# The diagonal of a linear-attention score block as eight products of its own, with a re-ordered start, hand-over and end

## The chip, the cores and the metric

The kernel runs on one core of one Trainium2 chip. The metric is the device time of one execution in microseconds (us), of the core; lower is better. PE is TensorE (PEld its weight loads), DVE VectorE, ACT ScalarE, POOL GpSimd, SP SyncE, which issues nearly all DMAs here.

## The reference

Two stages. The first is a recurrent attention with decay, over 4 batches, 8 heads, 768 steps and head width 48:

```
for t in range(S):
    cur = einsum('bhd,bhe->bhde', u * k[t], v[t])
    y[t] = einsum('bhd,bhde->bhe', r[t], state + cur)
    state = w * state + einsum('bhd,bhe->bhde', k[t], v[t])
```

The second is a mixture of eight experts on the 3072 x 384 result x. A token takes part where `x @ w_skip > 0`; its expert e is the largest of `x @ w_gate`, its weight g the softmax value there:

```
out = x;   out[tokens of e] += g * (relu(x @ w1[e]) @ w2[e])      # w1: 384 x 1024, w2: 1024 x 384
```

## The kernel before

**Attention.** The 768 steps are cut into 12 chunks of 64; two batches go together, so there are 24 steps `n` (two passes of 12), each with 8 heads as four pairs (`hp`) of two halves (`a`) of the 128 partitions, and two batches (`q`). Step `n` needs `dm[n]` (r and k, 512 KB) and `vz[n]` (v), both loaded on SP. DVE multiplies r by decay powers (`prep_r`, L412, writes `rd`), POOL multiplies k by the inverse powers (`prep_k`, L430, writes `kd`). The scores inside a chunk are `kd` against `rd`: below the diagonal with decay, on the diagonal with `u` in place of the decay. For the diagonal, `rd` holds a second copy of r that is multiplied by `uw` (u times w): two head pairs of it by DVE (L420), two by ACT (`bonus`, L406). `scores` (L442) makes 16 products of 64 x 64 weights and 128 moving columns: 64 for the copy below the diagonal, 64 for the diagonal's. Of the latter only the diagonal entries are used. Two predicated copies put both into `am`: L463 (`below`), L464 (`eye`).

A pass of the main loop (L890 on), for index `n`, writes in this order, which is the order on each engine: loads of `dm[n+5]`, `v[n+4]` and a piece of expert weights; `scores(n+1)`; the two masks; `across(n+1)` (L528, state against `rd`); a split of a weight piece (L115 on ACT, then L116 on POOL); `bonus(n+2)`; `turn_k(n+2)` (L455, transposes of `kd`); `turn_x(n)` (L571); `prep_k(n+3)`; a step or more of the routing (small DVE work); `prep_r(n+3)`; `state(n+1)` (L475); `within(n+1)` (L504, `am` against v); `evac(n+1)`, whose output goes back to DRAM on SP. Ahead of the loop the same is written out for steps 0 to 2, with `grow` (L325) making the powers for three more chunk positions, one of them on POOL.

**Routing and experts.** The router (`route`) sorts tokens into two lists of ids for each expert, 128 and 104 long (CAP = 232), in four groups of steps; the last group (`last`) can be done only after the last chunk. `gather(q)` (L124, indirect DMA on POOL) fetches a list's rows, `scatter(q)` (L174) writes them back. Weights are split into two parts, `hi` (ACT, L115) and `lo` (DVE or POOL, L116), and each product is made three times. Expert 0's two lists are run by `single`, a generator with 12 parts, so that they can be mixed into other work: `first` (list 0) is begun while the routing ends, `second` (list E) follows once gathered. The string `PLAN` gives the order: `a` a part of `first`, `B` a part of `second`, `x` the transposes of one list of expert 1, `s` a split, `u` a piece of expert 1, `g` a gather. `mix` (L171) adds an expert's result to its rows. Experts 1 to 7 are then run whole by `expert`.

**End.** Two flags are read on every engine (L1086, L1087) and two branches stand one behind the other (L1088, L1090) over code that is run only for unusual inputs.

Of the kernel before, what the change touches and what calls it, by code (L numbers as in the profile page):

```python
# [61 lines left out]
def tile_wkv_moe(  # L62
# [110 lines left out]
    def scatter(q):  # L173
        ins = nc.gpsimd.indirect_dma_start(  # L174
            out=out,
            out_offset=bass.IndirectOffsetOnAxis(ap=sid[:, q : q + 1], axis=0),
            in_=xs.pop(q),
            in_offset=None,
            bounds_check=N - 1,
            oob_is_err=False,  # L180
        )
# [64 lines left out]
    with ExitStack() as actx:  # L246
# [7 lines left out]
        def warm(k):  # L254
            for _ in range(k):
                nc.tensor.matmul(ps_t, ones[:, :P], ones, start=True, stop=True)
# [146 lines left out]
        def bonus(n, first=0):
            for hp in range(first, NHP):
                rd = rds[n][:, hp]
                nc.scalar.mul(rd[:, :, 1], rd[:, :, 0], uw[:, hp : hp + 1])  # L406

        def prep_r(n, parts=(0, 1)):
# [1 line left out]
            if 0 in parts:  # L410
                rds[n] = wk.tile([DR, NHP, 2, 2, C], F32, tag="rd", name=f"rd{n}", bufs=4)
                nc.vector.tensor_tensor(  # L412
                    rds[n][:, :, :, 0],
                    d[:, 0],
                    w_d[:, n % NSUB, 0][:, :, None].to_broadcast([DR, NHP, 2, C]),
                    ALU.mult,
                )
            if 1 in parts:
                rd = rds[n]
                nc.vector.tensor_tensor(  # L420
                    rd[:, :BH, :, 1],
                    rd[:, :BH, :, 0],
                    uw[:, :BH, None, None].to_broadcast([DR, BH, 2, C]),
                    ALU.mult,
                )
# [11 lines left out]
        def scores(n):  # L437
            kd, rd = kds.pop(n), rds[n]
            for hp in range(NHP):
                for a, q in FOUR:  # L440
# [1 line left out]
                    nc.tensor.matmul(  # L442
                        ps_p[q * C : (q + 1) * C, a, 2 * hp * C : 2 * (hp + 1) * C],
                        kd[h, hp, q, :],
                        rd[h, hp, q].rearrange("p s c -> p (s c)"),
# [13 lines left out]

        def mask_scores(n):  # L460
            p = ps_p.rearrange("p a (h s c) -> p (a h) s c", s=2, c=C)
            shape = lambda t: t.rearrange("p a (h c) -> p (a h) c", c=C)
            nc.vector.copy_predicated(shape(am[n % 2]), below, p[:, :, 0])  # L463
            nc.vector.copy_predicated(shape(am[n % 2]), eye, p[:, :, 1])  # L464
# [853 lines left out]
```

## Time and profile before

| | us |
|---|---|
| three runs | 267.34, 269.15, 269.96; median 269.15 |
| profiled execution | 267.03, its span 265.2 |
| start of the span to the third `scores` | 15.60 |
| from there to the last turn of the attention's result (L571) | 97.8 |
| hand-over from there to the flip of `second`'s first half (L208) | 18.3 |
| experts from there to the last product | 126.9 |
| behind the last product | 6.6 |

1.83 us of the profiled execution lie outside of its span. Over the whole span PE is busy 94%, DVE 71%, ACT 53%, POOL 50%; those are means over stages with different limits, so the stages have to be read one by one. A row of the timeline gives start, length, engine, line, operation, output and inputs, count, and in brackets how long the engine had been idle and what ended that. The granted TensorE clock is 0.993 of full speed.

### The profile page before, as it was taken

The page shows a single profiled execution, that of the slowest core. Times are in us where ns is not written, and L with a number is a line of the kernel's source. Part 1 is how long each engine was busy: PE and PEld are TensorE (multiplying, and loading weights), DVE is VectorE, ACT ScalarE, POOL GpSimd, SP SyncE. Part 2 cuts the span into 40 slices and gives each one's busy share as a digit, 9 for nine tenths or more (in the row PEclk, how much of TensorE's full clock was granted, in tenths as well). Part 3 has the DMA queues.
Part 4 walks back from the last instruction along what each step waited for, and adds up shares of the span by engine and source line. Part 5 has one row for each costly group of instructions (what it writes and reads, how often), then busy time and mean ns, then how long its engine had stood idle before and what let it go on. Part 6 is the DMA issues. An engine that isn't in the chain of part 4 may idle for free.

```text
span 265.2 us, 8834 instructions
## 1 busy us (share of the span) xinstructions
PE 249.3 (94%) x3594; PEld 229.0 (86%) x3594; DVE 188.9 (71%) x364; ACT 139.7 (53%) x314; POOL 131.9 (50%) x130
## 2 busy tenths in 40 slices
PE   7899999989899999898899999999999999999990
PEld 2799898878798889677698999999999999999990
DVE  8997477897899999674466986998478385692300
ACT  2566658766574766334566707548176282670200
POOL 8666325555655546304785944655535445345011
PEclk9999999999999999999999999999999999999997
DMA  6969798988888887557698796688838566001010
GB/s 213 303 181 259 207 278 248 289 252 244 266 232 264 241 267 205 159 156 262 204 313 261 244 320 230 205 275 253 253 105 279 157 201 222 23 1 46 0 36 24
DMA packets 31142, 54.22 MB, mean 204 GB/s; under 512 B 4536, under 2 KB 14413, under 8 KB 31089
## 3 DMA queue, kind: packets, MB, share of 16 engines
q1 hardware_dynamic: 28896, 48.09, 59.4%
q0 software_dynamic: 2048, 5.44, 6.6%
q8 instruction: 31, 0.51, 0.8%
q14 instruction: 23, 0.18, 0.3%
q10 hardware_dynamic: 144, 0.00, 0.0%
HBM read 45.72 MB, written 8.65 MB: 205 GB/s over the span
## 4 chain that ended last, share of the span: by engine, by line
PE 59%; DVE 8%; DMA 4%; issue 3%; POOL 2%; ACT 1%; SPq 1%; POOLq 0%
PE ps_p L166 11%; PE ps_y L166 11%; PE ps_y L156 5%; PE ps_p L156 5%; PE ps_r L156 5%; PE ps_l L156 5%; PE ps_p L442 3%; PE ps_y L504 2%; DMA dm<-in_dm_dram 2%; DMA raw<-in_w_dram 2%; PE ps_y L218 2%; PE ps_s L475 2%; DVE am L463 1%; DVE ol L768 1%; PE ps_l L455 1%
## 5 line engine op out<-in xcount | busy, mean ns | idle before, releaser
L116 POOL TENSOR_TENSOR lo<-raw,hi 128x512 fp32r<-128x512 f32 x40 | 53.7, 1348 | 43.9 <-ACT hi L115 42.0
L115 ACT CAST hi<-raw 128x512 fp32r<-128x512 f32 x96 | 54.7, 624 | 1.1 <-DMA raw<-in_w_dram 1.1
L116 DVE TENSOR_TENSOR lo<-raw,hi 128x512 fp32r<-128x512 f32 x56 | 50.5, 926 | 2.3 <-ACT hi L115 1.9
L430 POOL TENSOR_TENSOR kd<-dm,w_d 128x512 f32<-128x512 f32 x23 | 33.4, 1455 | 27.2 <-DMA dm<-in_dm_dram 17.8
L174 POOL DMA_INDIRECT out_dram<-xg,sid x16 | 16.8, 1052 | 38.0 <-DVE xg L171 25.7
L124 POOL DMA_INDIRECT xg<-out_dram,gid x16 | 18.1, 1132 | 17.7 <-DMA raw<-in_w_dram 11.9
L442 PE MATMUL ps_p<-rd,kd 64*64 64x128 f32 x768 | 26.7, 276 | 0.1
L463 DVE COPY_PREDICATED am<-below,ps_p 128x512 f32<-128x512 int8 x24 | 17.7, 736 | 11.6 <-PE ps_p L442 11.4
L442 PEld LDWEIGHTS ps_p<-rd,kd 64*64 64x64 f32 x768 | 20.8, 132 | 3.6 <-issue 1.5
L160 ACT ACTIVATE hh<-ps_p 128x464 fp32r<-128x464 f32 x7 | 3.9, 559 | 37.3 <-PE ps_p L156 22.5
L504 PE MATMUL ps_y<-vz,am 128*64 128x96 f32 x384 | 20.4, 248 | 2.3 <-DVE lists L783 0.9
L406 ACT ACTIVATE rd<-rd,uw 128x128 f32<-128x128 f32 x50 | 17.2, 395 | 6.3 <-DVE rd L412 6.1
L457 ACT COPY kt<-ps_l 128x512 f32<-128x512 f32 x22 | 12.9, 586 | 14.3 <-PE ps_l L455 14.1
L504 PEld LDWEIGHTS ps_y<-vz,am 128*64 128x64 f32 x384 | 17.3, 137 | 3.6 <-DVE am L464 1.1
L412 DVE TENSOR_TENSOR rd<-dm,w_d 128x512 f32<-128x512 f32 x24 | 18.8, 782 | 2.2 <-DMA dm<-in_dm_dram 2.2
L475 PE MATMUL ps_s<-vz,kt 128*64 128x96 f32 x352 | 19.6, 252 | 0.0
L166 PE MATMUL ps_p<-hi,hh 128*128 128x384 f32 x56 | 19.4, 347 | 0.0
L166 PE MATMUL ps_p<-hi,hl 128*128 128x384 f32 x56 | 19.0, 339 | 0.0
L166 PE MATMUL ps_y<-hi,hh 128*104 128x384 f32 x56 | 18.9, 338 | 0.0
L166 PE MATMUL ps_y<-lo,hh 128*104 128x384 f32 x56 | 18.9, 337 | 0.0
L166 PE MATMUL ps_y<-hi,hl 128*104 128x384 f32 x56 | 18.9, 337 | 0.0
L166 PE MATMUL ps_p<-lo,hh 128*128 128x384 f32 x56 | 18.8, 336 | 0.0
(239 smaller groups left out, 668.2 us busy)
## 6 DMA issues: line engine op xcount, KB each, us to landing
raw<-in_w_dram SPq DMA_DIRECT2D x96, 256.0 KB
dm<-in_dm_dram SPq DMA_DIRECT2D x24, 512.0 KB
vz<-in_tok_dram SPq DMA_DIRECT2D x48, 96.0 KB
out_dram<-xt SPq DMA_DIRECT2D x48, 96.0 KB
out_dram<-xt SPq DMA_DIRECT2D x4, 192.0 KB
xg<-out_dram,gid POOLq DMA_INDIRECT x16
out_dram<-xg,sid POOLq DMA_INDIRECT x16
wgp<-in_wgq_dram SPq DMA_DIRECT2D x1, 96.0 KB
```

The source lines that it names most:

```text
L115: nc.scalar.copy(hi, t)
L116: eng.tensor_tensor(lo, t, hi.bitcast(F32), ALU.subtract)
L124: ins = nc.gpsimd.indirect_dma_start(out=xg, out_offset=None, in_=out[0:rows], in_offset=bass.IndirectOffsetOnAxis(ap=gid[:, q : q + 1], a ...
L156: nc.tensor.matmul(ph, a[:, c, fs], b[:, c, :], start=(k == 0), stop=(k == 3 * NCC - 1))
L166: nc.tensor.matmul(py, a, b[:, f, :], start=(k == 0), stop=(k == 3 * NFC - 1))
L406: nc.scalar.mul(rd[:, :, 1], rd[:, :, 0], uw[:, hp : hp + 1])
L412: nc.vector.tensor_tensor(rds[n][:, :, :, 0], d[:, 0], w_d[:, n % NSUB, 0][:, :, None].to_broadcast([DR, NHP, 2, C]), ALU.mult,)
L430: (eng or nc.gpsimd).tensor_tensor(kds[n], d[:, 1], w_d[:, n % NSUB, 1][:, :, None].to_broadcast([DR, NHP, 2, C]), ALU.mult,)
L442: nc.tensor.matmul(ps_p[q * C : (q + 1) * C, a, 2 * hp * C : 2 * (hp + 1) * C], kd[h, hp, q, :], rd[h, hp, q].rearrange("p s c -> p (s c)" ...
L463: nc.vector.copy_predicated(shape(am[n % 2]), below, p[:, :, 0])
L475: nc.tensor.matmul(s[a * C : (a + 1) * C, :, hp * D : (hp + 1) * D], kt[:, hp, a, :], t[:, :, a, hp, :], start=i == 0 and hp == 0, stop=Tr ...
L504: ins = nc.tensor.matmul(place_y(a, c)[:, :, g, :], am[n % 2][:, a, hp * C : (hp + 1) * C], t[:, :, a, hp, :], start=g == 0 and n % NSTEP ...
```

## The change

Scores: `rd` is no longer doubled and `scores` moves 64 columns, not 128. The diagonal comes from `pair`, the product `rd * kd` elementwise (128 x 512, on DVE; on POOL for steps 0, 13, 17 and 21), and from a new `bonus`: eight products with 64 columns of `pair` as weights (all 128 partitions) and 2 moving columns, `uw`, which now holds u*w of the two halves in two columns with zeros elsewhere. They land in eight columns of `ps_p`, `own`, and `mask_own` copies them, broadcast over 64 columns, through `eye`. ACT has no `bonus` any more, DVE no L420. In the loop `pair(n+2)` stands behind the masks, and `bonus(n+2)` between `within(n+1)` and `scores(n+2)`. Ahead of the loop `uw` is made on POOL, the order is new, and five warm-up products stand there in place of one.

Hand-over: the last routing list is finished one part of `first` earlier (six products, L218); expert 1's first transposes come one part of `second` earlier; in `expert` the `yield` stands ahead of the splits, by which the mix of list E comes ahead of a split on DVE. Gathers and scatters of the second lists name 104 rows. End: the second branch now lies inside the first's body, and the outer one is on the flag that covers both.

```diff
-PLAN = "aasBsaBBBxasBxsgaBBgusBgsBguBBgBs"
+PLAN = "aaasBsaBBxBasBxsgaBBgusBgsBguBBgBs"
...
+ASIDE = (13, 17, 21)
...
+    def listed(q):
+        return P if q <= E else CAP - P
...
-            out=xg,
+            out=xg[:m],
...
-            in_offset=bass.IndirectOffsetOnAxis(ap=gid[:, q : q + 1], axis=0),
+            in_offset=bass.IndirectOffsetOnAxis(ap=gid[:m, q : q + 1], axis=0),
...
-        uw = tab.tile([DR, NHP], F32, name="uw")
-        nc.vector.tensor_tensor(uw, ub_sb, pw[:, 0, :NHP], ALU.mult)
+        uw = tab.tile([DR, NHP, 2], F32, name="uw")
+        nc.gpsimd.memset(uw, 0.0)
+        for a in range(2):
+            h = slice(a * C, (a + 1) * C)
+            nc.gpsimd.tensor_tensor(uw[h, :, a], ub_sb[h], pw[h, 0, :NHP], ALU.mult)
...
+        def pair(n, eng=None):
+            pds[n] = wk.tile([DR, NHP, 2, C], F32, tag="pd", name=f"pd{n}", bufs=3)
+            (eng or nc.vector).tensor_tensor(pds[n], rds[n], kds[n], ALU.mult)
+
+        own = ps_p[:, 0, C : C + 2 * NHP]
+
+        def bonus(n):
+            pd = pds.pop(n)
+            for hp in range(NHP):
+                for q in range(NB):
+                    nc.tensor.matmul(
+                        own[q * C : (q + 1) * C].rearrange("p (a h) -> p a h", a=2)[:, :, hp],
+                        pd[:, hp, q, :],
+                        uw[:, hp, :],
+                        start=True,
+                        stop=True,
+                    )
...
-                        ps_p[q * C : (q + 1) * C, a, 2 * hp * C : 2 * (hp + 1) * C],
+                        ps_p[q * C : (q + 1) * C, a, 2 * hp * C : (2 * hp + 1) * C],
                         kd[h, hp, q, :],
-                        rd[h, hp, q].rearrange("p s c -> p (s c)"),
+                        rd[h, hp, q, :],
...
+        def mask_own(n):
+            t = am[n % 2].rearrange("p a (h c) -> p (a h) c", c=C)
+            nc.vector.copy_predicated(t, eye, own.unsqueeze(2).to_broadcast([P, 2 * NHP, C]))
...
         prep_r(0)
-        bonus(0, BH)
         prep_k(0, nc.vector)
         grow(1)
+        pair(0, nc.gpsimd)
...
         scores(0)
-        prep_r(1, (0,))
+        warm(2)
+        bonus(0)
+        mask_scores(0)
+        mask_own(0)
+        prep_r(1)
         prep_k(1)
-        bonus(1)
         grow(2, nc.gpsimd)
-        mask_scores(0)
...
+        pair(1)
         prep_r(2)
-        bonus(2, BH)
...
             mask_scores(n + 1)
+            if n:
+                mask_own(n + 1)
...
-            if 0 < n and n + 2 < NT:
-                bonus(n + 2, BH)
+            if n + 2 < NT and n + 2 not in ASIDE:
+                pair(n + 2)
...
-                prep_r(n + 3, (0,))
+                prep_r(n + 3)
+                if n + 3 in ASIDE:
+                    pair(n + 3, nc.gpsimd)
             back = state(n + 1)
-            if n + 3 < NT:
-                prep_r(n + 3, (1,))
+            if n == 0:
+                bonus(1)
+                mask_own(1)
...
             within(n + 1, kcopy.get(n + 2, xcopy[n]))
+            if n + 2 < NT:
+                bonus(n + 2)
...
-        run(3)
+        run(2)
         both(last)
...
                 rectify(ph, hh[:, f0 : f0 + 2, :], hl[:, f0 : f0 + 2, :])
+                yield
                 split_next(2)
-                yield
...
-    with tc.If(redo_v > 0):
-        recompute_x(tc, dm, tok, wd, ub, out, bank)
     with tc.If(any_v > 0):
+        with tc.If(redo_v > 0):
+            recompute_x(tc, dm, tok, wd, ub, out, bank)
         remaining_tokens(tc, wg, w12, out, over, redo, ident, bank)
```

On DVE ahead of the loop and in its first pass, from `grow(1)` to the masks of step 1. Before (`rd_233` is step 1, `rd_277` step 2, `rd_333` step 3; `am_149` step 0, `am_150` step 1):

```order
L412 TENSOR_TENSOR rd_233<-dm_133,w_d 128x8x64
L463 COPY_PREDICATED am_149<-below,ps_p 128x512
L464 COPY_PREDICATED am_149<-eye,ps_p 128x512
L412 TENSOR_TENSOR rd_277<-dm_137,w_d 128x8x64
L420 TENSOR_TENSOR rd_277<-rd_277,uw 128x4x64
L325 TENSOR_TENSOR w_d<-w_d,pw 128x512
L463 COPY_PREDICATED am_150<-below,ps_p 128x512
L464 COPY_PREDICATED am_150<-eye,ps_p 128x512
```

The same place now (`rd_246`, `rd_288`, `rd_342` are steps 1, 2, 3; `pd_286`, `pd_328` the pairs of steps 1 and 2):

```order
L478 COPY_PREDICATED am_149<-below,ps_p 128x512
L473 COPY_PREDICATED am_149<-eye,ps_p 128x512
L413 TENSOR_TENSOR rd_246<-dm_133,w_d 128x512
L422 TENSOR_TENSOR pd_286<-rd_246,kd_248 128x512
L413 TENSOR_TENSOR rd_288<-dm_137,w_d 128x512
L329 TENSOR_TENSOR w_d<-w_d,pw 128x512
L478 COPY_PREDICATED am_150<-below,ps_p 128x512
L422 TENSOR_TENSOR pd_328<-rd_288,kd_290 128x512
L413 TENSOR_TENSOR rd_342<-dm_141,w_d 128x512
L473 COPY_PREDICATED am_150<-eye,ps_p 128x512
```

`rd` of step 1 stood ahead of the masks of step 0 and now stands behind them; between the two masks of step 1 now lie `pair` of step 2 and `rd` of step 3. POOL works through this at the same place (before: the same rows without the first two):

```order
L361 TENSOR_TENSOR uw<-ub_sb,pw 64x4 x2
L422 TENSOR_TENSOR pd_208<-rd_203,kd_205 128x512
L441 TENSOR_TENSOR kd_248<-dm_133,w_d 128x512
L329 TENSOR_TENSOR w_d<-w_d,pw 128x512
L441 TENSOR_TENSOR kd_290<-dm_137,w_d 128x512
L441 TENSOR_TENSOR kd_340<-dm_141,w_d 128x512
L441 TENSOR_TENSOR kd_432<-dm_251,w_d 128x512
```

A product of step 0's pair (`pd_208`) and the two of `uw` have moved ahead of every `kd` of POOL; the POOL `grow` (L329) lies between `kd` of step 1 and of step 2, as before. In the loop, on PE, one pass now reads:

```order
L453 MATMUL ps_p<-rd_342,kd_340 64x64 x16
L542 MATMUL ps_y<-sblk_200,rd_342 64x48 x16
L466 MATMUL ps_l<-ident,kd_432 128x128 x4
L585 MATMUL ps_t<-ident,xt_461 128x128 x3
L489 MATMUL ps_s<-vz_130,kt_426 64x2x48 x8
L518 MATMUL ps_y<-vz_130,am_150 64x2x48 x8
L430 MATMUL ps_p<-uw,pd_517 64x2 x8
```

The last row is new, and the first moved 64x128 before; nothing else on PE has moved within a pass.

More of the change, by code (lines that the diff above doesn't have):

```diff
@@ L43 @@
 GB = 4
-BH = 2
 NDM = 4
@@ L175, in scatter @@
             out=out,
-            out_offset=bass.IndirectOffsetOnAxis(ap=sid[:, q : q + 1], axis=0),
-            in_=xs.pop(q),
+            out_offset=bass.IndirectOffsetOnAxis(ap=sid[: listed(q), q : q + 1], axis=0),
+            in_=xs.pop(q)[: listed(q)],
             in_offset=None,
@@ L255, in warm @@
             for _ in range(k):
-                nc.tensor.matmul(ps_t, ones[:, :P], ones, start=True, stop=True)
+                nc.tensor.matmul(ps_r, ones[:, :P], ones, start=True, stop=True)
         warm(NWARM)
@@ L398, in setup_routes, with prep_r @@
             )
-        rds, kds, kts, kcopy = {}, {}, {}, {}
+        rds, kds, kts, kcopy, pds = {}, {}, {}, {}, {}
         FOUR = ((0, 0), (1, 1), (0, 1), (1, 0))
[L403 to L408, printed above, removed]
-            d = loaded[n][0]
[L410 to L425, printed above, removed]
+        def prep_r(n):
+            d = loaded[n][0]
+            rds[n] = wk.tile([DR, NHP, 2, C], F32, tag="rd", name=f"rd{n}", bufs=4)
+            nc.vector.tensor_tensor(
+                rds[n],
+                d[:, 0],
+                w_d[:, n % NSUB, 0][:, :, None].to_broadcast([DR, NHP, 2, C]),
+                ALU.mult,
+            )
[13 more added lines that the diff above has]
+                        stop=True,
+                    )
         def prep_k(n, eng=None):
@@ L458, in turn_k @@
             kts[n] = kt
+        def mask_own(n):
+            t = am[n % 2].rearrange("p a (h c) -> p (a h) c", c=C)
+            nc.vector.copy_predicated(t, eye, own.unsqueeze(2).to_broadcast([P, 2 * NHP, C]))
         def mask_scores(n):
             p = ps_p.rearrange("p a (h s c) -> p (a h) s c", s=2, c=C)
-            shape = lambda t: t.rearrange("p a (h c) -> p (a h) c", c=C)
-            nc.vector.copy_predicated(shape(am[n % 2]), below, p[:, :, 0])
-            nc.vector.copy_predicated(shape(am[n % 2]), eye, p[:, :, 1])
+            t = am[n % 2].rearrange("p a (h c) -> p (a h) c", c=C)
+            nc.vector.copy_predicated(t, below, p[:, :, 0])
         def state(n):
@@ L529, in across @@
                                 place_y(a, c)[:, q, g, :],
-                                rd[h, hp, q, 0, :],
+                                rd[h, hp, q, :],
                                 sblk[n % 2][h, q, hp * D : (hp + 1) * D],
@@ L871, in tile_wkv_moe @@
         scores(0)
-        prep_r(1, (0,))
+        warm(2)
[3 more added lines that the diff above has]
+        prep_r(1)
         prep_k(1)
-        bonus(1)
         grow(2, nc.gpsimd)
-        mask_scores(0)
         load_dm(4)
         state(0)
+        warm(2)
+        within(0)
+        evac(0)
         turn_k(1)
         warm(1)
-        within(0)
-        evac(0)
         load_v(4)
         nc.sync.dma_start(out=wgp, in_=wgq)
+        pair(1)
         prep_r(2)
-        bonus(2, BH)
         prep_k(2)
```

1 line of the change is left out of this document (added).

## The prediction

> **What bounds the kernel now.** First the page's sums, then the busy time of each engine stage by stage (stretch, its length, then busy us of PE, PEld, DVE, ACT and POOL, granted clock, share of DMA, GB/s):
>
> ```profile
> PE 249.3 (94%) x3594; PEld 229.0 (86%) x3594; DVE 188.9 (71%) x364; ACT 139.7 (53%) x314; POOL 131.9 (50%) x130
> 15.60:113.40 97.80, 93.44 (x2384) 82.80 (x2382) 81.11 (x164) 62.24 (x153) 49.86 (x46) 1.00 0.83 241
> 113.40:131.70 18.30, 16.31 (x107) 13.82 (x107) 9.32 (x40) 7.70 (x21) 7.61 (x7) 1.00 0.68 209
> 131.70:258.60 126.90, 126.24 (x915) 123.72 (x915) 83.84 (x125) 62.57 (x125) 61.44 (x51) 1.00 0.56 181
> ```
>
> PE bounds the loop (idle 97.80 − 93.44 = 4.36 us) and the experts (idle 0.66); in the hand-over it is idle for 1.99. So an edit in the loop is worth what it does to PE's work in a pass, and at most 4.4 us beyond that. One pass, in time order (start, length, ...):
>
> ```profile
> 19.47 1.10 PE L442 MATMUL ps_p<-rd,kd 64*64 64x128 f32 x32
> 20.39 0.63 PE L528 MATMUL ps_y<-sblk,rd 64*64 64x48 f32 x32
> 20.64 0.74 DVE L463 COPY_PREDICATED am<-below,ps_p 128x512 f32<-128x512 int8 x1 [0.54 <-PE ps_p L442]
> 20.95 0.66 PE L455 MATMUL ps_l<-ident,kd 128*128 128x128 f32 x4
> 21.41 0.74 DVE L464 COPY_PREDICATED am<-eye,ps_p 128x512 f32<-128x512 int8 x1
> 22.58 0.83 PE L504 MATMUL ps_y<-vz,am 128*64 128x96 f32 x16
> 23.34 1.10 PE L442 MATMUL ps_p<-rd,kd 64*64 64x128 f32 x32
> ```
>
> A pass is 23.34 − 19.47 = 3.87 us without a gap on PE, and DVE waits for `scores`. Ahead of the loop nothing is so dense; there the chain of single operations decides:
>
> ```profile
> 3.34 3.59 POOL L319 MEMSET vz<- 64x384 f32 x8
> 7.44 1.32 POOL L430 TENSOR_TENSOR kd<-dm,w_d 128x512 f32<-128x512 f32 x1 [0.51 <-POOL vz L319]
> 7.51 1.80 DVE L412 TENSOR_TENSOR rd<-dm,w_d 128x512 f32<-128x512 f32 x1
> 8.73 1.49 POOL L325 TENSOR_TENSOR w_d<-w_d,pw 128x512 f32<-128x512 f32 x1
> 10.06 0.73 DVE L464 COPY_PREDICATED am<-eye,ps_p 128x512 f32<-128x512 int8 x1
> 10.29 1.30 POOL L430 TENSOR_TENSOR kd<-dm,w_d 128x512 f32<-128x512 f32 x1
> 10.69 1.45 DVE L412 TENSOR_TENSOR rd<-dm,w_d 128x512 f32<-128x512 f32 x1
> 11.66 1.10 PE L442 MATMUL ps_p<-rd,kd 64*64 64x128 f32 x32
> 12.52 0.68 DVE L325 TENSOR_TENSOR w_d<-w_d,pw 128x512 f32<-128x512 f32 x1
> 13.12 0.73 DVE L463 COPY_PREDICATED am<-below,ps_p 128x512 f32<-128x512 int8 x1
> 13.28 3.10 POOL L430 TENSOR_TENSOR kd<-dm,w_d 128x512 f32<-128x512 f32 x2 [1.69 <-DVE w_d L325]
> 15.60 1.10 PE L442 MATMUL ps_p<-rd,kd 64*64 64x128 f32 x32
> ```
>
> A DVE product of two SBUF tensors takes 0.68 us when POOL is idle (12.52). Begun within a POOL product it takes 1.80 or 1.45: POOL's end (8.76, 11.59) plus 0.55. POOL's next is then stretched by some 0.2 (1.49 against 1.30). Masks, which read PSUM, don't suffer (0.73 beside POOL's at 10.06).
>
> **The start: +4.4 us (bounds +1.5 and +5.4).** `pair` adds such DVE products to a place where POOL works without a gap, and `own` of step 1, for which `within` waits, now stands behind `pair(2)` and `rd` of step 3. I replay it with these lengths. POOL is free at 6.93, the two small `uw` products take it to 7.4 (no row; 0.2 each, estimated from the gap), `pair(0)` runs to 8.7, `kd(1)` to 10.0, `grow(2)` to 11.3. PE does `bonus(0)` by 9.25, DVE its mask 9.45 to 10.2. `rd(1)` now meets `grow(2)`: done at 11.85, `scores(1)` at 11.95 (before 11.66). `pair(1)` meets `kd(2)`, stretched to 12.8: 13.35. `rd(2)` is free, since POOL's `kd(3)` waits for `grow(3)`: 14.05, and `grow(3)` 14.75. The mask `below(1)` ends at 15.5 (before 13.85). `pair(2)` meets `kd(3)` (14.85 to 16.15): 16.7; `rd(3)` meets `kd(4)` (to 17.65): 18.2; `own(1)` 18.95. Then 0.76 for `within` (23.34 − 22.58) and 0.5 for `bonus(2)`: the third `scores` starts at 20.25 instead of 15.60, 4.65 later. Had the mask of step 0 ended just before 10.0, `rd(1)` would slip in ahead of `grow(2)` and the same chain ends 0.65 earlier, +4.0; I take +4.4, near the worse branch. With no meeting at all the eight DVE steps behind 10.2 take 8 × 0.7 = 5.6 and the third `scores` comes at 17.1, +1.5; one more meeting costs 0.77 (1.45 − 0.68), +5.4. Later work doesn't hide the delay, since the loop has only its 4.36 of idle.
>
> **A pass on PE: +0.8 us (bounds −0.9 and +12).** `scores` takes 20.39 − 19.47 = 0.92 for 32 records, some 27 ns apart. `across` has equal weights (64 x 64) and 48 columns: last start 0.22 before the stage's end, so 32 starts in 0.41, 13 apart. With 64 columns I take half the present pace, 0.43 plus 0.06 of change-over: 0.49, a gain of 0.43 in 22 passes, −9.5. `bonus` has 16 records of 128 x 64 weights on alternating column halves with almost nothing to move. In `across` one of the four tiles reloads every 4 × 13 = 53 ns; two tiles then give 27 apart, 16 × 27 + 60 = 0.49, in 21 passes +10.3. The lower bound has it at 0.41, the whole of `across`'s starts. The upper is a row whose weights all go to one place:
>
> ```profile
> 114.96 0.77 PEld L581 LDWEIGHTS ps_y<-wgp,xT 128*64 128x64 f32 x12 [0.37 <-ACT lg L618]
> ```
>
> 64 ns each, 1.03 a pass, +11.3 more. I take the two-tile value: `within` (128 x 64, 16 records in 0.76, 48 apart with 96 columns to move) is the nearest row in shape, and it loads beside running products (one by one its 16 loads alone would take 1.03). [...]
>
> **DVE in the loop: 0 (bounds −4.4 and +4.5).** Groups of the loop (busy, mean ns | idle before):
>
> ```profile
> L420 DVE TENSOR_TENSOR rd<-rd,uw 128x256 f32<-128x256 f32 x22 | 17.7, 803 | 0.6
> L463 DVE COPY_PREDICATED am<-below,ps_p 128x512 f32<-128x512 int8 x23 | 16.9, 737 | 11.6 <-PE ps_p L442 11.4
> L412 DVE TENSOR_TENSOR rd<-dm,w_d 128x512 f32<-128x512 f32 x22 | 16.3, 740 | 2.2 <-DMA dm<-in_dm_dram 2.2
> ```
>
> L420 goes: 0.80, of which about half is waiting for POOL. `pair` comes in 18 passes at the place that L412 has now, right behind the masks, where it rarely meets POOL (740 against 680); `rd` moves to a later place. In a pass `pair` ends 0.75 (0.49, and 0.25 as from 20.39 to 20.64) + 0.74 + 0.74 + 0.7 = 2.95 behind the start of `scores`, and `bonus` asks for it at 3.45 less a little: 0.45 of slack. In some passes the masks are late now:
>
> ```profile
> 79.77 1.10 PE L442 MATMUL ps_p<-rd,kd 64*64 64x128 f32 x32
> 81.30 1.38 DVE L420 TENSOR_TENSOR rd<-rd,uw 128x256 f32<-128x256 f32 x1
> 82.61 0.72 DVE L463 COPY_PREDICATED am<-below,ps_p 128x512 f32<-128x512 int8 x1
> ```
>
> Without L420 this mask could start 1.3 earlier; against it, `pair` and its 0.69 stand in the same queue, and `rd` inherits L420's place. If every such wait went, the gain is the loop's whole idle, 4.36. If `pair` met POOL as often as L420 does (some 9 in 22, at 0.95 each, less the slack): 9 × 0.5 = +4.5. ACT loses its part (off the path), three pairs on POOL lie a pass ahead of their use.
>
> **Hand-over: −1.8 (bounds −2.3 and −0.5).** PE's waits there, and the length of a part (six products, from the chain):
>
> ```profile
> 126.43 0.55 PE L147 MATMUL ps_t<-ident,xg 128*128 128x128 f32 x3 [1.23 <-DMA xg<-out_dram,gid]
> 131.69 0.66 PE L208 MATMUL ps_s<-ident,h 128*128 128x128 f32 x4 [0.46 <-DVE xl L149]
> 135.73 1.05 PE ps_y L218 x6
> 142.99 1.38 DVE L116 TENSOR_TENSOR lo<-raw,hi 128x512 fp32r<-128x512 f32 x1 [0.38 <-ACT hi L115]
> 144.95 0.38 PE L156 MATMUL ps_y<-xh,hi 128*128 128x232 f32 x1 [0.59 <-issue]
> ```
>
> The last list goes ahead of six products, so its gather starts up to 1.05 earlier and 0.9 of 1.23 should go. The transposes one part earlier give `xl` time: 0.4 of 0.46. At 144.95 PE stands behind a mix that DVE begins after the split at 142.99; ahead of that split it is early: 0.5 of 0.59. All three whole: 2.3; if the list then waits for DVE's routing instead, 0.5 is left. Splits now stand behind the `yield`, but the experts' 0.66 of idle says that weights come in time.
>
> **End: −0.2 (bounds −0.2 and 0).**
>
> ```profile
> 259.54 0.97 POOL L174 DMA_INDIRECT out_dram<-xg,sid  x1 [3.23 <-DVE xg L171]
> L1312 POOLq DRAIN  x3: 40/107/3392, 261.0 to 264.9; - x3
> ```
>
> POOL's last scatter and its drain of 3.39 set the end. 104 of 128 rows save at most 24/128 × 0.97 = 0.18; the branch that goes lies beside the drain.
>
> **Sum:** 4.4 + 0.8 + 0 − 1.8 − 0.2 = +3.2 on the profiled 267.03 (1.83 of it outside the span): 270.2. That execution is 2.1 below the median of the runs, so against the median 269.15: 272.3.
>
> **The rivals.** *Masks on time* (the other side): the freed L420 lets DVE stay ahead in the passes with late masks, and PE loses its 4.36 of idle: 272.3 − 4.4 = 267.9, not slower. It decides if `pair` stays within its 0.45 of slack where POOL splits. For it: 0.38 us of waiting in each L420. Against: DVE has 0.27 more to do in a pass when nothing collides (0.69 against 0.42). *A clean start*: POOL and DVE happen to interleave, +1.5 in place of +4.4: 269.4. Against it stand the two rows of 1.80 and 1.45. *Both*: 265.0. *Loads one by one*: 272.3 + 11.3 = 283.6. *A slower clock behind the new gap*: the replay leaves PE idle from some 15.1, when `bonus(1)` is through, to 19.0. PE does begin slowly: its loads come 0.43 apart up to 5.35 (one more lies between these rows), then 0.21 (5 in 1.05):
>
> ```profile
> 4.49 0.15 PEld L256 LDWEIGHTS <-ones 128*128 128x128 bf16 x1 [0.27 <-issue]
> 5.35 1.05 PEld L256 LDWEIGHTS <-ones 128*128 128x128 bf16 x5 [0.28 <-issue]
> ```
>
> If a gap of 3.9 sets it back to half pace for one pass (3.87), of which half is lost: +1.9, 274.2. [...]
>
> **How the numbers follow.** Forecast 0.45; masks on time 0.15; clean start 0.15; both 0.10; loads one by one 0.06; clock 0.09. One per cent, about what a measurement here can tell, is 2.7 us: 266.5 to 271.8. Faster by more: both (0.09), the better end of masks on time (0.04), 0.01 of the clean start: 0.14. Within: 0.10 of masks on time, 0.12 of the clean start, 0.01 of both, and 0.15 of the forecast, whose own range is 270 to 275: 0.38. Slower takes the rest, 0.48. The range 266.0 to 277.0 leaves out the serial loads, most of "both" and the outer bounds of the loop's terms, some 0.19.
>
> **What would show it.** The third `scores` near 20.2, with DVE products of 1.2 us and more ahead of it, and PE waiting for DVE at `within(1)`; a steady pass of 3.9 with `scores` and `bonus` near 0.5 each; no wait of 1.2 for the second list's rows. I am wrong if the third `scores` comes before 18, if `bonus` takes 0.7 or more, or if PE's idle time in the loop moves by more than 2 us.

## The result

Slower: 281.27 us median (280.09 to 282.62, 4 runs) against 269.55 (267.34 to 270.77, 4 runs), a ratio of 1.0446 with a 95% interval of 1.0389 to 1.0504, 11.7 us. The forecast was 272.3, within 266.0 to 277.0. The sign was right; the loss of 11.7 is 3.7 times the 3.2 of the forecast.

The profiled execution of the changed kernel took 282.42, one of its slower ones, and that of the kernel before 267.03, one of its faster ones. Their spans differ by 15.5, and the table splits that. It comes from the windows below.

| stage | before | after | difference | forecast |
|---|---|---|---|---|
| start of the span to the third `scores` | 15.60 | 20.96 | +5.36 | +4.4 |
| the pass behind it | 3.87 | 6.27 | +2.40 | 0 (a rival: +1.9) |
| fourth `scores` to the attention's last turn | 93.96 | 100.08 | +6.12 | +0.8 |
| from there to the last product | 145.18 | 146.66 | +1.48 | −1.8 |
| behind the last product | 6.59 | 6.73 | +0.14 | −0.2 |

### The profile page after: what moved, and what is told of

It reads as the page before. It is cut to its first block, busy times and chain, and to the rows that moved or that the text cites. A ratio compares the mean times of both kernels' runs of the same rounds, so it can differ in the third digit from the quotient of the medians.

```text
span 280.7 us, 9550 instructions
## 1 busy us (share of the span) xinstructions
PE 257.1 (92%) x3980; PEld 236.8 (84%) x3982; DVE 192.1 (68%) x360; ACT 124.8 (44%) x264; POOL 138.3 (49%) x137
## 4 chain that ended last, share of the span: by engine, by line
PE 74%; DVE 13%; issue 4%; DMA 4%; POOL 3%; ACT 1%; SPq 0%; POOLq 0%; DVEq 0%
PE ps_p L170 11%; PE ps_y L170 10%; PE ps_p L160 5%; PE ps_r L160 5%; PE ps_l L160 5%; PE ps_y L160 5%; PE ps_p L453 5%; PE ps_y L518 5%; PE ps_p L430 4%; PE ps_s L489 3%; PE ps_l L466 3%; DVE pd L422 3%; DVE am L473 3%; DVE am L478 3%; PE ps_y L542 3%
## 5 line engine op out<-in xcount | busy, mean ns | idle before, releaser
L116 DVE TENSOR_TENSOR lo<-raw,hi 128x512 fp32r<-128x512 f32 x56 | 51.8, 950 | 2.4 <-ACT hi L115 2.2
L441 POOL TENSOR_TENSOR kd<-dm,w_d 128x512 f32<-128x512 f32 x23 | 34.6, 1510 | 17.9 <-DMA dm<-in_dm_dram 12.7
L178 POOL DMA_INDIRECT out_dram<-xg,sid x16 | 17.6, 1100 | 36.7 <-DVE xg L175 28.5
L518 PE MATMUL ps_y<-vz,am 128*64 128x96 f32 x384 | 21.0, 252 | 4.3 <-DVE am L473 4.1
L422 DVE TENSOR_TENSOR pd<-rd,kd 128x512 f32<-128x512 f32 x20 | 21.2, 1060 | 0.1
L453 PE MATMUL ps_p<-rd,kd 64*64 64x64 f32 x768 | 17.7, 228 | 1.1 <-issue 0.9
L430 PEld LDWEIGHTS ps_p<-uw,pd 128*64 128x64 f32 x384 | 14.5, 141 | 4.9 <-DVE pd L422 2.4
L489 PEld LDWEIGHTS ps_s<-vz,kt 128*64 128x64 f32 x352 | 15.8, 140 | 3.3 <-issue 3.2
```

Source lines behind the costliest of these rows:

```text
L116: eng.tensor_tensor(lo, t, hi.bitcast(F32), ALU.subtract)
L422: (eng or nc.vector).tensor_tensor(pds[n], rds[n], kds[n], ALU.mult)
L430: nc.tensor.matmul(own[q * C : (q + 1) * C].rearrange("p (a h) -> p a h", a=2)[:, :, hp], pd[:, hp, q, :], uw[:, hp, :], start=True, stop= ...
L441: (eng or nc.gpsimd).tensor_tensor(kds[n], d[:, 1], w_d[:, n % NSUB, 1][:, :, None].to_broadcast([DR, NHP, 2, C]), ALU.mult,)
L453: nc.tensor.matmul(ps_p[q * C : (q + 1) * C, a, 2 * hp * C : (2 * hp + 1) * C], kd[h, hp, q, :], rd[h, hp, q, :], start=True, stop=True,)
L489: nc.tensor.matmul(s[a * C : (a + 1) * C, :, hp * D : (hp + 1) * D], kt[:, hp, a, :], t[:, :, a, hp, :], start=i == 0 and hp == 0, stop=Tr ...
```

## The profile after

The same stages of the changed kernel (stretch, length, busy us of PE, PEld, DVE, ACT, POOL, granted clock, share of DMA, GB/s), and then the row of the granted clock, 40 slices of 7.0 us:

```profile
0.00:20.96 20.96, 15.48 (x241) 10.42 (x244) 14.89 (x34) 5.34 (x9) 16.31 (x38) 0.96 0.72 213
20.96:27.23 6.27, 6.27 (x120) 5.83 (x119) 3.31 (x10) 1.83 (x4) 2.39 (x6) 0.58 0.57 149
27.23:127.31 100.08, 91.82 (x2604) 82.19 (x2600) 79.38 (x152) 47.35 (x108) 48.20 (x37) 1.00 0.76 219
127.31:273.97 146.66, 143.53 (x1021) 138.37 (x1021) 93.90 (x164) 70.30 (x145) 70.39 (x57) 0.99 0.57 181
273.97:280.70 6.73, 0.00 (x1) 0.00 (x0) 0.62 (x1) 0.00 (x0) 1.02 (x1) 0.86 0.08 21
PEclk9986999999999999999979999999999999999998
```

Before, the third of these stages had PE busy for 89.57 of 93.96: so of the +6.12 in the loop 2.25 lies in PE's busy time and 3.87 in its idle time. Not all of the 2.25 is work: a wait shows in part as busy (at 34.99, below, the eight products are 0.52 late, of which 0.35 is idle time), and the same products are busy for only 90.06 where the pair products are left out (experiment 4). Of the idle time 1.4 ends with `pair`, and 3.8 (1.6 before) ends with nothing that the profile shows ("issue"). The clock stands at 0.58 in the second stage; the row shows a second, smaller dip in slice 21 (140 to 147 us). The start, in time order:

```profile
9.61 0.74 DVE L478 COPY_PREDICATED am<-below,ps_p 128x512 f32<-128x512 int8 x1 [2.50 <-PE ps_p L430]
10.02 1.05 POOL L329 TENSOR_TENSOR w_d<-w_d,pw 128x512 f32<-128x512 f32 x1
11.07 0.67 DVE L413 TENSOR_TENSOR rd<-dm,w_d 128x512 f32<-128x512 f32 x1
11.15 1.76 POOL L441 TENSOR_TENSOR kd<-dm,w_d 128x512 f32<-128x512 f32 x1
11.85 1.61 DVE L422 TENSOR_TENSOR pd<-rd,kd 128x512 f32<-128x512 f32 x1
14.74 2.98 POOL L441 TENSOR_TENSOR kd<-dm,w_d 128x512 f32<-128x512 f32 x2 [1.83 <-DVE w_d L329]
15.21 1.39 DVE L422 TENSOR_TENSOR pd<-rd,kd 128x512 f32<-128x512 f32 x1
16.52 1.74 DVE L413 TENSOR_TENSOR rd<-dm,w_d 128x512 f32<-128x512 f32 x1
18.19 0.71 DVE L473 COPY_PREDICATED am<-eye,ps_p 128x512 f32<-128x512 int8 x1
19.05 1.23 PE L518 MATMUL ps_y<-vz,am 128*64 128x96 f32 x16 [2.92 <-DVE am L473]
20.00 1.03 PE L430 MATMUL ps_p<-uw,pd 128*64 128x2 f32 x16
20.96 1.14 PE L453 MATMUL ps_p<-rd,kd 64*64 64x64 f32 x32
```

`pair(1)`, `pair(2)` and `rd` of step 3 meet POOL (1.61, 1.39, 1.74 against 0.68), and the diagonal's mask of step 1 is done at 18.90; the replay had 18.95. Ahead of `pair(1)` the replay was off twice, and the two errors cancel: the mask below the diagonal of step 0 waited for the eight products (9.61), which the replay left out, and so `rd` of step 1 began at 11.07, just as POOL's `grow` ended, and met nothing (0.67). Behind PE's wait of 2.92, `within`, the eight products and `scores` take 1.23, 1.03 and 1.14. At full clock they are 0.83, 0.58 and 0.69, as the first undisturbed pass shows:

```profile
27.23 0.69 PE L453 MATMUL ps_p<-rd,kd 64*64 64x64 f32 x32
27.75 0.63 PE L542 MATMUL ps_y<-sblk,rd 64*64 64x48 f32 x32
29.94 0.83 PE L518 MATMUL ps_y<-vz,am 128*64 128x96 f32 x16
30.60 0.58 PE L430 MATMUL ps_p<-uw,pd 128*64 128x2 f32 x16
31.11 0.69 PE L453 MATMUL ps_p<-rd,kd 64*64 64x64 f32 x32
```

The stages of this pass are 27.75 − 27.23 = 0.52 for `scores` and 31.11 − 30.60 = 0.51 for `bonus` (0.49 each in the forecast). `within` gives way to what follows it after 30.60 − 29.94 = 0.66, where before it was 0.76, and so the whole pass is 3.88 (3.87 before). In the next pass, the pair product, and below it the group of them from the fourth `scores` to the last turn:

```profile
33.07 1.31 POOL L441 TENSOR_TENSOR kd<-dm,w_d 128x512 f32<-128x512 f32 x1 [4.79 <-DMA dm<-in_dm_dram]
33.27 1.67 DVE L422 TENSOR_TENSOR pd<-rd,kd 128x512 f32<-128x512 f32 x1
34.99 0.63 PE L430 MATMUL ps_p<-uw,pd 128*64 128x2 f32 x16 [0.35 <-DVE pd L422]
L422 DVE TENSOR_TENSOR pd<-rd,kd 128x512 f32<-128x512 f32 x17 | 17.5, 1031 | 0.0
```

`kd` starts when its load has landed, just ahead of `pair`, which then takes 1.67, and PE waits. Over the loop `pair` takes 1031 ns on average, 1.37 to 1.77 us in six of its 17 passes; the forecast put the 740 that the operation in this place had before. The eight products, which follow `within` by 0.66 when nothing is late, are 0.2 to 0.9 us late in five passes, 2.4 in all: that is PE's own wait for `pair`.

## The experiments

The changed kernel's theory after this comparison: the start's order makes the delay, PE's idle time there lets the clock fall, and in the loop it is the pair products that cost.

**1. The idle time of PE filled** (changed kernel):

```diff
             if n == 0:
                 bonus(1)
+                warm(13)
                 mask_own(1)
```

> The changed kernel with 13 more warm-up products in PE's idle time ahead of within(1). Theory (PE's idle time of 2.9 us lets the clock fall): the granted clock stays at 1.0, the pass behind the third scores takes 3.9 us instead of 6.27, within(1) and the eight products run at full pace, 2.5 to 3 us in all: about 278.4. Rival (the slow stretch has another source, such as transfers): no change, 281.

Measured: 277.28 (277.08 to 279.56), ratio to before on the same chip 1.0391 (1.0307 to 1.0475). Windows of its profile, from the third `scores` and from the fourth on:

```profile
20.41:24.28 3.87, 3.87 (x122) 3.63 (x119) 3.04 (x8) 1.92 (x5) 2.98 (x5) 1.00 0.44 91
24.28:124.78 100.50, 92.21 (x2605) 82.48 (x2601) 82.41 (x156) 47.60 (x108) 50.25 (x37) 1.00 0.76 224
```

The slow pass is gone, 3.87 in place of 6.27, and the fourth `scores` comes 2.95 earlier (24.28, 27.23). The loop still takes 100.3 (the second window ends 0.17 behind the last turn).

**2. A gap alone, in the kernel before**: step 1's two masks four times over.

```diff
             scores(n + 1)
-            mask_scores(n + 1)
+            for _ in range(1 if n else 4):
+                mask_scores(n + 1)
```

> The kernel before with step 1's two masks done four times over in place of once: 6 masks more, 4.4 us of DVE, PE idle meanwhile. Theory (a gap on PE of 3 us and more is enough for the clock to fall): third scores near 20, a slow pass or two behind it, 2 us and more on top of the delay: loop's end 7 us late, 275. Rival (the clock falls because of the new kind of products): no slow pass, only the delay: 272.5.

Measured: 274.29 (272.54 to 275.91), ratio 1.0171 (1.0081 to 1.0261).

```profile
19.49 1.31 PE L504 MATMUL ps_y<-vz,am 128*64 128x96 f32 x16 [4.39 <-DVE am L464]
20.73 1.99 PE L442 MATMUL ps_p<-rd,kd 64*64 64x128 f32 x32
20.73:25.76 5.03, 5.03 (x105) 4.69 (x104) 2.84 (x9) 2.52 (x6) 2.45 (x5) 0.75 0.41 103
25.76:119.32 93.56, 89.59 (x2281) 79.53 (x2280) 79.39 (x156) 59.46 (x148) 46.01 (x34) 1.00 0.82 238
```

Without any of the new products the clock falls behind the gap (0.75; the 1.10 of `scores` becomes 1.99), so idle time is enough to cause it; the wait here is 4.39, longer than the 2.92 of the changed kernel. And a start that is 6.3 late (25.76 against 19.47) leaves the loop at 93.56, as before: being late cost the loop nothing in this profile.

The same delay with 21 warm-up products in the gap:

```diff
+            if n == 0:
+                warm(21)
             within(n + 1, kcopy.get(n + 2, xcopy[n]))
```

> The same, with 21 warm-up products in the gap. Theory (the delay alone doesn't disturb the loop): full clock, delay of 4.4 to 5 us, and 94 us from the fourth scores to the loop's end as before: 273. Rival (a late start lets the loads come late for the whole loop): 96 to 99 us, 275 to 278.

Measured: 268.59 to 276.35, too far apart for a ratio. In its profile the pass behind the third `scores` takes 3.87, and the loop from the fourth on 95.2, between the two expectations; the kernel before and its variants need 93.6 to 96.1 there over the five profiles of this study, so this decides nothing.

**3. The start in another order** (changed kernel): the diagonal's work of step 1 ahead.

```diff
             across(n + 1)
+            if n == 0:
+                bonus(1)
+                mask_own(1)
...
             back = state(n + 1)
-            if n == 0:
-                bonus(1)
-                mask_own(1)
```

> The changed kernel, but the eight products of step 1 and their mask stand ahead of the pair of step 2 and of rd of step 3. Theory (the order of the start is the source): the third scores comes near 17.4 instead of 20.96, PE has no wait near 3 us there, the clock stays full in the pass behind it (3.9 us instead of 6.27), together about 6 us: 275. If the loop's waits between the 5th and 15th pass come only from being late with the loads, they shrink too and the time is 270 to 273. Rival (the loop loses its 5 us by itself): 275, and the loop's passes from the 4th on as long as in the changed kernel.

Measured: 276.71 (275.09 to 280.33), ratio 1.0324 (1.0242 to 1.0406). The third `scores` came at 20.56 and not near 17.4. The reason is clearer in the next kernel, which has this edit, the pair of step 0 on DVE, `rd` of step 1 ahead of step 0's masks, `rd` of step 2 ahead of step 1's pair, the transposes of step 1's `kd` ahead of `within(0)`, and three warm-ups less. The lines for the second and the third of these:

```diff
-        pair(0, nc.gpsimd)
+        pair(0)
...
+        prep_r(1)
+        prep_k(1)
+        grow(2, nc.gpsimd)
         mask_scores(0)
         mask_own(0)
-        prep_r(1)
-        prep_k(1)
-        grow(2, nc.gpsimd)
```

> The changed kernel with another order ahead of the loop: the pair of step 0 on DVE in place of POOL, rd of step 1 ahead of step 0's masks as in the kernel before, step 1's eight products and their mask right behind across(1). Theory 1 (the order of the start makes the delay): the third scores near 16.2 (20.96 in the changed kernel), no slow pass behind it: 7 us less at the fourth scores. For the loop: if pair meets POOL's kd whatever the start, the loop still loses some 4 us to before and the time is about 274; rival (being late with the loads makes them meet): the loop's loss goes too, about 270.

Measured: 278.39 (276.03 to 279.58), ratio 1.0363 (1.0269 to 1.0457). Its third `scores` at 20.25 misses the 16.2 by far. PE's row of the eight products of step 1, and its windows of the start:

```profile
14.26 0.87 PE L430 MATMUL ps_p<-uw,pd 128*64 128x2 f32 x16 [1.51 <-DVE am L478]
11.40:14.20 2.80, 1.35 (x66) 1.11 (x64) 2.80 (x3) 0.48 (x1) 1.57 (x2) 1.00 0.85 243
14.48:24.72 10.24, 10.24 (x153) 9.46 (x152) 5.42 (x12) 3.09 (x6) 5.63 (x13) 0.50 0.58 156
```

The eight products wait here for the mask below the diagonal, which reads the tile `ps_p` that they write. Behind 1.45 us of idle time in 2.80 the clock is at half for 10.2 us, and that is what eats the earlier start. With 7 warm-up products ahead of these eight:

```diff
             if n == 0:
+                warm(7)
                 bonus(1)
```

> The kernel with the faster start (pair of step 0 on DVE, rd of step 1 ahead of the masks, step 1's eight products early), and 7 warm-up products more ahead of step 1's eight products, where PE was idle for 1.5 us. Theory (PE's idle time between 11.4 and 14.2 is what lets the clock fall to 0.52 behind it): the clock stays at 1.0, the third scores comes near 17.0, the fourth near 20.9 (26.12 without the warm-ups). Then the loop: if it loses 6 us whatever the start, the loop takes 100 from the fourth scores on and the time is about 273; rival (lateness makes the loop's loss): 95 to 97 and 269.

Measured: 277.80 (274.90 to 278.91), ratio 1.0295 (1.0211 to 1.0379). In the profiled execution (274.90):

```profile
0.00:17.89 17.89, 15.72 (x247) 10.07 (x247) 14.60 (x35) 5.15 (x9) 14.88 (x35) 1.00 0.76 221
17.89:21.77 3.88, 3.88 (x124) 3.64 (x120) 3.01 (x9) 1.93 (x5) 0.26 (x2) 1.00 0.72 199
21.77:122.76 100.99, 92.25 (x2604) 82.27 (x2600) 82.10 (x154) 47.44 (x108) 52.19 (x42) 1.00 0.77 223
```

The clock stays at 1.00 and the start loses 2.3 instead of 7.8 (21.77 against 19.47). The loop still takes 101: the loop's loss has nothing to do with the start. The other executions of this kernel show mean clocks of 0.987, 0.976 and 0.973 and times of 277.2, 278.5 and 278.9; where in them the clock fell is not on record.

**4. The loop without its pair products** (changed kernel; the pairs of steps 3 and on are left out, and their eight products read step 1's pair):

```diff
-            if n + 2 < NT and n + 2 not in ASIDE:
-                pair(n + 2)
+            if n == 0:
+                pair(2)
+            elif n + 2 < NT:
+                pds[n + 2] = first
...
-                if n + 3 in ASIDE:
-                    pair(n + 3, nc.gpsimd)
```

> The changed kernel without the pair products of steps 3 and on; the eight products of these steps use step 1's pair, so the diagonal is wrong from there. Theory (pair meets POOL's kd and comes late, and PE waits for it): the waits of the 5th to 15th pass go, 3.6 to 5 us less, 276 to 277.5. Rival (the eight products themselves or late loads): no change beyond 1 us, 280 to 281.

Measured: 274.92 (274.18 to 278.42), ratio 1.0321 (1.0219 to 1.0422). Its window from the fourth `scores` to the last turn:

```profile
25.99:121.84 95.85, 90.06 (x2604) 81.98 (x2600) 68.86 (x135) 47.64 (x107) 44.01 (x34) 1.00 0.79 229
```

With pair and its wait the loop takes 100.08 (100.33, 99.76 and 100.99 in the profiles of experiments 1 and 3; 103.69 in the first kernel of experiment 3, whose mean clock was 0.972, against 0.995 in experiment 1). Without pair 95.85: 4.2 is the pair's. The 1.9 over the 93.96 of before are not the eight products' own time, since an undisturbed pass is as long as before (3.88 and 3.87): PE is busy 0.5 longer and idle 1.4 longer, and of its idle time 5.0 is "issue", against 1.6. These waits come to 0.2 to 4.7 in the profiles of the kernel before and its variants, and the loop with 4.7 of them takes 96.1; in the changed kernel and those of its variants whose loop ran at full clock they are 2.4 to 5.2. Why they are more was not tried.

To split the 4.2, two kernels put something back in pair's place on DVE, again with step 1's pair for the eight products: the product itself, written to a tile that nobody reads, or a second copy of the diagonal's mask.

```diff
             elif n + 2 < NT:
                 pds[n + 2] = first
+                if n + 2 not in ASIDE:
+                    nc.vector.tensor_tensor(spare, rds[n + 2], kds[n + 2], ALU.mult)
```

> The same, with the pair products done in their place on DVE but not read: the eight products use step 1's pair as in the kernel without pair (the diagonal is wrong). It has the meeting with POOL and DVE's time, but PE never waits for the product itself. If the loss is PE's wait for pair: 96 to 97 from the fourth scores to the loop's end, total 275. If it is what queues behind pair on DVE (masks, routing) or on POOL: 99 to 100, total 279.

Measured: 279.77 (277.64 to 283.26), ratio 1.0423 (1.0334 to 1.0512). The same window:

```profile
26.05:124.14 98.09, 90.73 (x2603) 82.22 (x2599) 79.03 (x152) 47.37 (x108) 46.41 (x34) 1.00 0.78 224
```

Its 98.09 lies between the expectations: some 2 of the 4.2 come back when PE doesn't wait for the product, as the 2.4 counted in the changed kernel's passes would have it. 2.2 stay, and that they are work that queues behind it on DVE and POOL is argued, not shown. Single profiles scatter by up to 2.5 us here, so the halves are rough, and its median, unlike its loop, is no better than that of the changed kernel's other variants.

```diff
+                if n + 2 not in ASIDE:
+                    mask_own(n + 1)
```

> The kernel without the pair products of steps 3 and on, with a second copy of the diagonal's mask in each one's place: the same time on DVE (0.74 against 0.69), but from PSUM, so that it doesn't meet POOL; the eight products don't wait for it (the diagonal is wrong as there). From the fourth scores to the loop's end the changed kernel takes 100, without pair 96. Theory (it is the meeting with POOL and the wait for it): stays at 96 to 97, total 275. Rival (DVE's time as such, which delays masks and routing behind it): 99 to 100, total 279.

Measured: 279.64 (277.97 to 280.24), ratio 1.04 (1.0328 to 1.0472); 100.7 from the fourth `scores` on. This one doesn't decide what it was made for: the second copy of the mask writes what `within` reads, so PE waited for it, 0.3 us in pass after pass.

**5. Pair ahead of the masks**, where DVE waits for `scores`:

```diff
             scores(n + 1)
+            if n and n + 2 < NT and n + 2 not in ASIDE:
+                pair(n + 2)
             mask_scores(n + 1)
...
-            if n + 2 < NT and n + 2 not in ASIDE:
+            if not n:
                 pair(n + 2)
```

> The changed kernel with the pair products of the loop ahead of the two masks, where DVE waits for PE's scores, in place of behind them. Theory (behind the masks pair meets kd on POOL, which starts when its load lands): mean of pair falls from 1.08 us toward 0.7, PE's waits at the eight products go, about 4 us less: 277. Rival (pair's work delays the masks wherever it stands): no change or slower, 281 and more.

Measured: 279.56 (278.11 to 280.92), ratio 1.0417 (1.0327 to 1.0507). Its group of pair products in the loop, its loop, and the windows of two passes:

```profile
L422 DVE TENSOR_TENSOR pd<-rd,kd 128x512 f32<-128x512 f32 x17 | 11.7, 690 | 1.5
26.01:128.58 102.57, 93.00 (x2604) 84.27 (x2600) 79.33 (x151) 47.26 (x108) 47.54 (x37) 0.97 0.75 215
44.70:50.60 5.90, 4.10 (x125) 3.77 (x123) 3.19 (x5) 2.37 (x5) 0.84 (x1) 1.00 0.79 243
50.60:56.80 6.20, 6.20 (x146) 5.56 (x145) 2.73 (x4) 2.02 (x4) 1.69 (x2) 0.72 0.95 285
```

The products no longer meet POOL (690 ns, as expected), PE no longer waits for them, and the loop is not faster, 102.57. That doesn't clear the meeting: the clock of this loop is 0.97, a pass with 1.8 us of idle PE ("issue") is followed by one at 0.72, and this hides what the move may have brought.

**6. The eight products twice** (from step 4 on):

```diff
-            for hp in range(NHP):
+            for hp in [*range(NHP)] * (2 if n > 3 else 1):
```

> The changed kernel with the eight products issued twice, from step 4 on (20 steps). At 0.5 us a set by the prediction's two-tile value, on the path in every pass: 20 x 0.5 = +10, 291. If the waits behind them hide a part: +5 to +8. Rival (weight loads one by one, 64 ns each): 20 x 1.03 = +20.

Measured: 289.31 (287.14 to 293.69), ratio 1.0747 (1.0644 to 1.0850).

```profile
26.78:136.92 110.14, 102.50 (x2923) 94.05 (x2919) 77.30 (x152) 47.37 (x108) 49.01 (x37) 0.97 0.70 199
30.14 1.05 PE L430 MATMUL ps_p<-uw,pd 128*64 128x2 f32 x32
```

110.14 − 100.08 = 10.1 for 20 sets, 0.50 each, with some of it from the clock (0.97 here, 1.00 there). The first doubled set shows the price at full clock: `scores` follows it at 31.12, so it takes 0.98 in place of 0.51, 0.47 more, near the two-tile price of the forecast. At the 64 ns of the row with all loads to one place, loads one by one would have been 20.6 more. They overlap here: a load of these products lasts 138 ns (the median; 132 to 231), and 32 of them fit into the 0.98.

**7. Hand-over and end, each alone in the kernel before.** First these three moves:

```diff
-PLAN = "aasBsaBBBxasBxsgaBBgusBgsBguBBgBs"
+PLAN = "aaasBsaBBxBasBxsgaBBgusBgsBguBBgBs"
...
-        run(3)
+        run(2)
...
+                yield
                 split_next(2)
-                yield
```

> The kernel before with nothing but the three moves of the hand-over (last list one part earlier, expert 1's transposes one part earlier, the yield ahead of the splits). By the prediction's step: 1.8 us less, 267.7 against 269.5, the wait for the second list's rows near 0.3 instead of 1.23. Rival (the rows take longer when they are asked for earlier, beside the weight loads, or the wait only moves): within 0.5 us of before.

Measured: 267.16 (264.94 to 271.05, 10 runs) against 268.31, ratio 0.9994 (0.9947 to 1.0040). From the attention's last turn to the last product:

```profile
113.65:257.76 144.11, 142.02 (x1021) 137.35 (x1021) 91.29 (x164) 70.37 (x145) 69.17 (x57) 1.00 0.57 186
126.98 0.55 PE L147 MATMUL ps_t<-ident,xg 128*128 128x128 f32 x3 [1.53 <-DMA xg<-out_dram,gid]
```

144.11 against 145.18, −1.1. The two later waits (0.46 and 0.59) are gone, the one for the second list's rows has not shrunk: 1.53 against 1.23. A gain of 0.4% lies within the interval of the timed runs.

Then the branches and the 104 rows, word for word as in the change:

```diff
-            in_offset=bass.IndirectOffsetOnAxis(ap=gid[:, q : q + 1], axis=0),
+            in_offset=bass.IndirectOffsetOnAxis(ap=gid[:m, q : q + 1], axis=0),
...
     with tc.If(any_v > 0):
+        with tc.If(redo_v > 0):
+            recompute_x(tc, dm, tok, wd, ub, out, bank)
```

> The kernel before with only the nested branches and 104 rows in the second lists' gathers and scatters. By the prediction's step: -0.2 us, not to be told from before. Rival (a branch less on every engine ends the program earlier): -0.5 to -1.

Measured: 268.67 (267.18 to 272.22, 10 runs) against 267.99, ratio 1.0061 (1.0016 to 1.0105): no gain. Behind the last product its profile has 6.9 us, against 6.6. It also bears on the hand-over:

```profile
116.32:260.41 144.09, 142.50 (x1021) 137.39 (x1021) 92.28 (x164) 70.31 (x145) 71.44 (x57) 1.00 0.59 184
```

From the last turn to the last product it takes 144.09, without the three moves, and here too the two later waits are gone. So that the moves took them away, and the −1.1 with them, isn't shown.

## Why the prediction was wrong

*The start* was right in its mechanism and in its length: from `pair(1)` on the replay is within 0.2 us at each operation, and at the mask that ends it 18.90 against 18.95. That it stands so near is in part luck, since of its two errors ahead of `pair(1)` one took back the other. The 5.36 at the third `scores` has 0.7 in it of products that already run at the lower clock.

*The clock* was listed as a rival of 0.09, "if a gap of 3.9 sets it back to half pace for one pass", +1.9. It came, with 2.92 of idle time, as +2.4 in the pass and 0.7 ahead of it. The step that failed is to set it beside the forecast as another case, though the replay's own gap was its cause: the two belong in one sum. Experiments 1 and 2 show it from both sides. The half pace was an estimate from PE's first loads (0.43 us apart, then 0.21); of a fall behind idle time the profile before has a case too, behind the last product, where PE idles for 6.6 us and the clock of the stretch is 0.72.

*A pass on PE: +0.8*: the two stages were taken as 0.49 and 0.49 and are 0.52 and 0.51, near enough, and the loads do overlap (16 within 0.51, where one lasts 138 ns). The sum left out that `within` gives way 0.10 sooner when the eight products follow it; an undisturbed pass is 0.01 longer than before, +0.2 over the loop.

*DVE in the loop: 0* is the step that failed most; it measured +4.2. "Right behind the masks, where it rarely meets POOL" was read from L412. In the kernel before:

```profile
70.10 0.69 DVE L412 TENSOR_TENSOR rd<-dm,w_d 128x512 f32<-128x512 f32 x1 [0.72 <-DMA dm<-in_dm_dram]
70.17 1.78 POOL L430 TENSOR_TENSOR kd<-dm,w_d 128x512 f32<-128x512 f32 x1 [1.19 <-DMA dm<-in_dm_dram]
70.83 1.41 DVE L420 TENSOR_TENSOR rd<-rd,uw 128x256 f32<-128x256 f32 x1
```

L412 waited for the same load as `kd` and got in just ahead of it; `kd` and L420 were the longer for it (1.78 and 1.41; the medians of their rows are 1.31 and 0.43). `pair` waits for no load, so a `kd` that has begun is in its way (1031 ns against 740). The bound of +4.5 was there, and the measured cost lies at it. By itself it would have stayed within the range (272.3 + 4.5 = 276.8), and so would the clock (274.2); the range had no room for both, and both came. The forecast's own sign of being wrong showed too: PE's idle time from the third `scores` to the last turn went from 4.4 to 8.3. Some 2.4 of the 4.2 are PE's wait for `pair`, as counted above; that the rest is work that queues on DVE is settled only roughly. The "issue" waits, some 2 us more in the loop than before (3.8 against 1.6), stood in no term, and their cause stays open.

*Hand-over: −1.8*: −1.1 in the kernel before with the moves, and −0.3 to −1.7 in nine profiles of the changed kernel's variants (144.93 to 143.46 against 145.18). The later waits went as forecast, but they went without the moves as well (experiment 7). For the first, the gather is asked for earlier, and the rows mostly don't come earlier: PE waits for them 0.5 to 1.8 in the variants, 1.23 before. In the profiled execution of the changed kernel it is the other way round, +1.48. The gather before, and then after with PE's wait and the clock behind it:

```profile
122.96 1.02 POOL L124 DMA_INDIRECT xg<-out_dram,gid  x1 [11.88 <-DMA raw<-in_w_dram]
```

```profile
135.80 1.02 POOL L128 DMA_INDIRECT xg<-out_dram,gid  x1 [11.24 <-DMA raw<-in_w_dram]
141.55 0.55 PE L151 MATMUL ps_t<-ident,xg 128*128 128x128 f32 x3 [2.43 <-DMA xg<-out_dram,gid]
141.50:148.00 6.50, 6.45 (x30) 5.33 (x30) 3.70 (x5) 2.66 (x7) 2.92 (x3) 0.74 0.71 219
```

The gather starts 8.5 behind the last turn (9.5 before) and its rows come 5.7 later (3.5 before), and behind PE's 2.43 of waiting the clock is 0.74. The longer wait and the slower clock behind it are enough for the difference to the variants. Why the rows took longer there was not tried.

*The end* is 0, as good as forecast.

## What to carry to other kernels

A gap that a forecast opens on PE has to be priced with the clock behind it in the same sum: here 2.9 us of idle time cost about 3 more. A new operation in an old one's place doesn't inherit its waits; ask what it is released by, and what the operation that it may meet (here POOL's `kd`) is released by. An edit that only exchanges work on the bounding engine (a pass of 3.87 for one of 3.88) has nothing to pay for what it adds on the engines beside it.
